# Twenty-three more identity products on TensorE around batch 0's second softmax

## The chip, the cores and the metric

The kernel runs on one core of a Trainium2 chip. The metric is the device time of one execution in microseconds, as the median over several runs. Beside it stands one profiled execution, whose trace gives each instruction's engine, start and duration. PE is TensorE, DVE VectorE, ACT ScalarE, POOL GpSimd, and SP the engine that issues the DMAs. PEld is TensorE's loading of weights.

## What is computed

Eight batches of eight heads, 576 tokens of 64 channels. Each head has 32 "packs" p, which first attend to the keys and values; the queries then attend to the packed result. What comes out, 4608 tokens of 512 channels, goes through a feed-forward layer with a hidden width of 2048.

```python
def sm_attn(qq, kk, vv):
    s = scale * np.matmul(qq, kk.transpose(0, 1, 3, 2))
    s = s - np.max(s, axis=-1, keepdims=True)
    a = np.exp(s)
    a = a / (np.sum(a, axis=-1, keepdims=True) + 1e-09)
    return np.matmul(a, vv)
p_packed = sm_attn(p, k, v)
out = sm_attn(q, p_packed, p_packed)
# x: out with its heads side by side, one row for each token
h = x @ w_in
g = h * (1.0 / (1.0 + np.exp(-h)))
return (g @ w_out).astype(np.float32)
```

The products that decide the length are done in three parts each: an operand is split into an upper and a lower half (`_hi`, `_lo`), and upper by upper, upper by lower and lower by upper are added up.

## The kernel before

For one batch the work goes like this. `scores1` multiplies packs by keys, `largest1`, `exps1` and `shares1` are the first softmax, `turned1` and `spread1` bring the exponentials to the other orientation, `packed` (L309) multiplies them by the values; for all batches but the first, `spread1` does its turn with 16 DMAs on SP (L288) behind two DVE transposes (L270). `scaled1`, `turned` and `packs` (L332, tile `ppT`) end this half. `scores2` multiplies queries by the packed result. For batch 0 it works in the orientation of the tokens (L350, in pieces of 32 columns), and then comes the second softmax in two halves: `less2` (the maximum, L387, and its subtraction, L388), `exps2` (L399 on ACT), `shares2` (sum L408, L409, L410, product L411), and `back2` turns the shares back by transposes on PE (L378, L380) into PSUM. `upper2` (L429, on ACT, tile `a_hi`) and `lower2` (L433, on DVE, tile `a_lo`) split them.

The packed result is not multiplied by the shares directly: `Packs` (`pp`) multiplies it by blocks of w_in (L211, `heads`, eight products), `pu` (L457 on ACT, `pw_hi`) and `pl` (L460 on DVE, `pw_lo`) split the result, and `h` (L488) multiplies shares and these blocks into hidden values; `g` (L506 to L508, ACT) applies the activation, `l` (L513, DVE) makes the lower half `g_lo`, and `o` (L520) multiplies by w_out into the output's sums. The weights come as 64-bit numbers and are taken apart and put together on ACT, DVE and POOL for the first 65 us or so (`ws`, `wz`, `wj`, `wu`, `wl`).

For the first two batches the order of all of this is written out by hand in the string `ORDER`: each word is a step, a letter or two for what it does, then its numbers. The words issue instructions on all the engines, and each engine runs its own in that order. `pp2`, `pu2`, `pl2` are the third block of packs; `aS0.0` is `scores2` of batch 0's first half, and `aM`, `aX`, `aD`, `aU`, `aH`, `aL` are `less2`, `exps2`, `shares2`, `back2`, `upper2`, `lower2`. A word `W` with a number n is `keep_warm(n)`:

```python
def two_banks():
    return ps_two.tile([P, 2, 512], F32, name="ps_two")
def keep_warm(n):
    ps = two_banks()
    for _ in range(n):
        nc.tensor.matmul(ps[:, 0, :P], ident, ident, start=True, stop=True)
```

That is n products of the 128x128 identity with itself into a PSUM tile that nobody reads (L132). Each of them shows as two records in the trace, as other f32 products do (L211, L309, L350). The pool `ps_two` has two buffers; the packs' products and the hidden products take theirs from it too. The kernel before has W2, W14, W12 and W5 in its first 20 us and W1 later.

Of the kernel before, what the change touches and what calls it, by code (L numbers as in the profile page):

```python
# [50 lines left out]
ORDER = """  # L51
wf0 ws0 wz0 k0 wf1 W2 wj0 as0.0 as0.1 wf2 ws1 am0.0 W14 ax0.0 am0.1 wf3 wz1 at0.0 v0 wj1 ax0.1 ay0.0 ws3 ws2
at0.1 W12 ay0.1 ar0 wz3 wu1 wz2 wj3 aa0 wf4 wj2 an0 W5 wl1 ai0 aj0 pp0 ws4 q0 pp1 wu3 wz4 pu0 aS0.0 wf5
aS0.1 wl3 wj4 wf6 wf7 pu1 pl0 pl1 aM0.0 wf8 pp2 pu2 aX0.0 pl2 ws7 aM0.1 k1 ws5 aD0.0 aX0.1 aU0.0 wf9 aD0.1
aU0.1 wz7 ws8 aH0.0 aL0.0 ws6 as1.0 aH0.1 wz8 wz5 ac1.0 q1 aL0.1 h0.0 wj5 wj7 as1.1 g0.0 ws9 ac1.1 h0.1 h1.0
l0.0 am1 g0.1 l0.1 wu5 o0.0 wu7 wz6 h1.1 g1.0 o0.1 v1 g1.1 wl5 wf10 l1.0 wl7 ax1.0 l1.1 wj6 o1.0 h2.0 ax1.1
o1.1 wz9 g2.0 wj8 h2.1 l2.0 at1.0 g2.1 pp3 pu3 pl3 at1.1 o2.0 l2.1 wj9 h3.0 ws10 o2.1 g3.0 ar1 h3.1 l3.0
wf11 ws11 pp4 o3.0 g3.1 pu4 wf12 wz10 ws12 l3.1 wj10 ay1 pl4 wz11 o3.1 wu10 wf13 h4 wj11 h5 wl10 g4 wu11 l4
aa1 o4 wz12 g5 an1 wl11 wf14 l5 ws13 ai1 aj1 h6 wj12 g6 wz13 aS1.0 o5 aT1.0 wj13 W1 ws14 h7 pp5 l6 o6 g7
wz14 aS1.1 wf15 pu5 l7 pl5 wj14 aT1.1 aM1.0 h8 g8 o7 wu14 wf16 k2 aM1.1 h9 ws15 l8 wl14 pp6 wz15 g9 aX1.0  # L60
aX1.1 wj15 l9 aD1.0 o8 h10 pu6 wu15 g10 pl6 o9 aH1.0 wl15 l10 v2 h11 o10 ws16 as2.0 g11 aL1.0 pp7 aD1.1
ac2.0 l11 pu7 as2.1 aH1.1 pl7 aL1.1 wf17 o11 h12 ws17 e11.0 g12 ac2.1 h13 e11.1 l12 g13 am2 h14 ax2.0 wz17
l13 wz16 h15 ax2.1 o12 g14 o13 l14 h16 wj16 g15 o14 l15 wj17 g16 wf18 ws18 h17 l16 o15 wz18 g17 l17 wf19
at2.0 h18 o16 at2.1 ws19 wj18 g18 h19 l18 o17 pp8 wu18 g19 q2 pu8 wz19 pl8 l19 ay2 o18 h20 g20 ar2 l20 o19
h21 wj19 o20 wl18 aa2 an2 g21 l21 pp9 h22 pu9 pl9 o21 h23 wu19 g22 l22 ai2 g23 aj2 wl19 o22 l23 h24 g24 o23
h25 aS2.0 l24 o24 g25 l25 aT2.0 h26 aS2.1 aM2.0 o25 g26 h27 l26 aT2.1 aM2.1 aX2.0 aX2.1 o26 pp10 g27 pp11 k3
pu10 aD2.0 l27 o27 pu11 pl10 pl11 e27.0 h28 e27.1 g28 l28 h29 g29 h30 v3 h31 o28 l29 aH2.0 aD2.1 aH2.1 o29
g30 l30 g31 l31 o30 g32 o31 aL2.1 l32 aL2.0 b0 e31.1 e31.0
"""


# [668 lines left out]
```

## Time and profile before

| | us |
|---|---|
| median of three runs | 716.32 |
| the three runs | 713.69, 716.32, 716.49 |
| the profiled execution | 713.68 |
| its span, first to last instruction | 711.9 |
| PE busy in the span | 695.0 |
| DVE busy | 332.7 |
| ACT busy | 325.0 |

A busy share is an average over stages with different limits, and the 712 us have two kinds of stage: the first 65 us, in which weights are prepared and attention of batches 0 and 1 is begun, and the rest. Where the change stands, the share of an engine in the stretch and the wait that ended last there have to be read. [...]

### The profile page before, as it was taken

The numbers are of one execution on the slowest core, as the hardware profiler recorded it, in microseconds if no ns is written. First come the engines' busy times: TensorE is split into PE (matmuls) and PEld (weight loads), VectorE is DVE, ScalarE is ACT, GpSimd is POOL, SyncE is SP. The second block draws the span as 40 slices with busy tenths as digits, with TensorE's granted clock in tenths as the row PEclk, the third lists the DMA queues.
The fourth block names the chain that finished last, engine by engine and source line by source line (L and its number), as shares of the span: only waits on it lengthen the run. The fifth ranks groups of instructions, "written<-read, shape, count | busy, mean of one in ns | idle before, by whom it ended". The sixth has DMA issues, their size and how long they took to land.

```text
span 711.9 us, 12319 instructions
## 1 busy us (share of the span) xinstructions
PE 695.0 (98%) x5170; PEld 570.4 (80%) x5170; DVE 332.7 (47%) x504; ACT 325.0 (46%) x612; POOL 18.7 (3%) x16
## 2 busy tenths in 40 slices
PE   7699999999999999999999999999999999999997
PEld 5477778887878887888878888878878888888886
DVE  5899986535543336332562325533362334622112
ACT  5597686434534425362542624453252532533221
POOL 1012110110000000000000000000000000000000
PEclk9789999999999999999999999999999999999999
DMA  9864714220512130212111121021301210010002
GB/s 341 355 229 129 293 65 188 87 71 1 185 60 82 34 139 0 100 44 89 67 60 54 43 90 68 21 106 35 137 1 60 82 35 1 1 60 1 1 1 74
DMA packets 30934, 62.07 MB, mean 87 GB/s; under 512 B 19360, under 2 KB 19360, under 8 KB 26528
## 3 DMA queue, kind: packets, MB, share of 16 engines
q1 hardware_dynamic: 30784, 61.16, 24.6%
q8 instruction: 41, 0.67, 0.4%
q10 hardware_dynamic: 96, 0.13, 0.1%
q14 instruction: 13, 0.11, 0.1%
HBM read 46.66 MB, written 10.49 MB: 80 GB/s over the span
## 4 chain that ended last, share of the span: by engine, by line
PE 94%; DVE 2%; SPq 1%; DMA 1%; issue 0%; ACT 0%; ACTq 0%
PE ps_acc L520 55%; PE ps_two L488 28%; PE ps_two L211 7%; PE ps_two L309 2%; SPq L288 1%; PE ps_two L132 1%; DMA kvq_t<-in_pkT 1%; PE ps_acc L350 1%; PE ps_acc L378 0%; DMA tm<-tm 0%; DVE g_lo L513 0%; PE ps_acc L309 0%; DVE tm L270 0%; DVE mx L247 0%; DVE w_raw L185 0%
## 5 line engine op out<-in xcount | busy, mean ns | idle before, releaser
L520 PE MATMUL ps_acc<-wo_hi,g_hi 128*128 128x512 f32 x576 | 229.3, 398 | 0.0
L520 PE MATMUL ps_acc<-wo_lo,g_hi 128*128 128x512 f32 x576 | 225.3, 391 | 0.0
L520 PE MATMUL ps_acc<-wo_hi,g_lo 128*128 128x512 f32 x576 | 225.0, 391 | 0.0
L513 DVE TENSOR_TENSOR g_lo<-g,g_hi 128x512 fp32r<-128x512 f32 (+1 forms) x132 | 90.9, 688 | 263.8 <-ACT g_hi L507 263.8
L506 ACT ACTIVATE g<-ps_two 128x512 f32<-128x512 f32 (+1 forms) x132 | 77.5, 587 | 275.8 <-PE ps_two L488 258.7
L488 PE MATMUL ps_two<-a_hi,pw_hi 128*128 128x288 f32 x512 | 153.2, 299 | 0.1
L488 PE MATMUL ps_two<-a_lo,pw_hi 128*128 128x288 f32 x512 | 152.0, 297 | 0.0
L488 PE MATMUL ps_two<-a_hi,pw_lo 128*128 128x288 f32 x512 | 151.2, 295 | 0.0
L520 PEld LDWEIGHTS ps_acc<-wo_hi,g_hi 128*128 128x128 f32 x576 | 108.0, 188 | 40.6 <-issue 21.0
L520 PEld LDWEIGHTS ps_acc<-wo_hi,g_lo 128*128 128x128 f32 x576 | 108.1, 188 | 24.0 <-DVE g_lo L513 0.5
L520 PEld LDWEIGHTS ps_acc<-wo_lo,g_hi 128*128 128x128 f32 x576 | 108.2, 188 | 18.2
L488 PEld LDWEIGHTS ps_two<-a_hi,pw_hi 128*128 128x128 f32 x512 | 96.9, 189 | 8.5 <-ACT rest L508 1.4
L488 PEld LDWEIGHTS ps_two<-a_lo,pw_hi 128*128 128x128 f32 x512 | 96.7, 189 | 3.6
L488 PEld LDWEIGHTS ps_two<-a_hi,pw_lo 128*128 128x128 f32 x512 | 96.7, 189 | 0.0
L507 ACT ACTIVATE g_hi<-ps_two 128x512 fp32r<-128x512 f32 (+1 forms) x132 | 76.6, 580 | 6.3 <-PE ps_acc L520 6.3
L460 DVE TENSOR_TENSOR pw_lo<-ps_two,pw_hi 128x1024 fp32r<-128x1024 f32 (+1 forms) x35 | 38.3, 1126 | 13.9 <-ACT pw_hi L457 13.9
L457 ACT CAST pw_hi<-ps_two 128x1024 fp32r<-128x1024 f32 (+1 forms) x35 | 31.7, 945 | 25.5 <-PE ps_two L211 25.5
L211 PE MATMUL ps_two<-win,ppT 64*32 64x512 f32 (+1 forms) x560 | 33.0, 559 | 1.1 <-issue 0.6
L508 ACT ACTIVATE rest<-ps_two 128x64 f32<-128x64 f32 (+1 forms) x132 | 30.2, 229 | 0.0
L211 PEld LDWEIGHTS ps_two<-win,ppT 64*32 64x32 f32 x560 | 8.2, 105 | 14.1 <-issue 11.2
L506 ACT ACT_TABLE_LOAD x15 | 19.2, 1283 | 0.5 <-PE ps_two L488 0.4
L498 ACT CAST g_hi<-rest 128x512 fp32r<-128x512 f32 x16 | 9.9, 624 | 14.5 <-PE ps_acc L520 14.2
(98 smaller groups left out, 446.3 us busy)
## 6 DMA issues: line engine op xcount, KB each, us to landing
kvq_t<-in_pkT SPq DMA_DIRECT2D x7, 1216.0 KB, 6.7
kvq_t<-in_vA SPq DMA_DIRECT2D x8, 1024.0 KB, 5.3
out<-o SPq DMA_DIRECT2D x16, 512.0 KB, 2.8
kvq_t<-in_qT SPq DMA_DIRECT2D x7, 1152.0 KB, 5.6
w_raw<-in_w_in SPq DMA_DIRECT2D x6, 1024.0 KB, 6.3
win<-in_w_out SPq DMA_DIRECT2D x3, 1024.0 KB, 4.9
w_raw<-in_w_out SPq DMA_DIRECT2D x3, 1024.0 KB, 4.8
tm<-tm SPq DMA_DIRECT2D x56, 40.0 KB, 2.0
```

What stands on the lines that cost most here:

```text
L132: nc.tensor.matmul(ps[:, 0, :P], ident, ident, start=True, stop=True)
L211: nc.tensor.matmul(bank(par)[NP * i : NP * i + NP], lhs(r, i), rhs(r, i), start=True, stop=True)
L309: nc.tensor.matmul(self.ps[NP * i : NP * i + NP, par * D : par * D + D], e, v[:n, c, h * D : h * D + D], start=(c == 0), stop=(c == 4),)
L457: nc.scalar.copy(self.hi, self.ps[:, :, : self.nf * P])
L460: nc.vector.tensor_tensor(self.lo, self.ps[:, :, : self.nf * P], self.hi.bitcast(F32), ALU.subtract)
L488: nc.tensor.matmul(bank, p[:, par, cols], a[:, par], start=(n == 0), stop=(n == len(todo) - 1))
L498: nc.scalar.copy(g_hi, g)
L506: nc.scalar.activation(g, ps[..., :MAIN], AF.Silu)
L507: nc.scalar.activation(g_hi, ps[..., :MAIN], AF.Silu)
L508: nc.scalar.activation(to, ps[..., MAIN:HS], AF.Silu)
L513: nc.vector.tensor_tensor(g_lo[:, c], g[:, c], g_hi[:, c].bitcast(F32), ALU.subtract)
L520: nc.tensor.matmul(bank, g[:, rows], w[:, f], start=(first and n == 0), stop=(last and n == 2))
```

## The change

Two words are put into `ORDER`: `W4` behind `wf8`, ahead of `pp2` (the third block of packs), and `W19` behind `aX0.1`, ahead of `aU0.0` (the transposes of the first half's shares). All other words stay in their order; the lines below are only broken in other places.

```diff
-aS0.1 wl3 wj4 wf6 wf7 pu1 pl0 pl1 aM0.0 wf8 pp2 pu2 aX0.0 pl2 ws7 aM0.1 k1 ws5 aD0.0 aX0.1 aU0.0 wf9 aD0.1
-aU0.1 wz7 ws8 aH0.0 aL0.0 ws6 as1.0 aH0.1 wz8 wz5 ac1.0 q1 aL0.1 h0.0 wj5 wj7 as1.1 g0.0 ws9 ac1.1 h0.1 h1.0
+aS0.1 wl3 wj4 wf6 wf7 pu1 pl0 pl1 aM0.0 wf8 W4 pp2 pu2 aX0.0 pl2 ws7 aM0.1 k1 ws5 aD0.0 aX0.1 W19 aU0.0 wf9
+aD0.1 aU0.1 wz7 ws8 aH0.0 aL0.0 ws6 as1.0 aH0.1 wz8 wz5 ac1.0 q1 aL0.1 h0.0 wj5 wj7 as1.1 g0.0 ws9 ac1.1
...
```

On PE, from the end of batch 0's second scores (L350) to its transposes (L378), this is the piece of the difference, with what each instruction waits for:

```order
 L350 MATMUL ps_acc<-ppT,kvq_t 128x32 x16
+L132 MATMUL ps_two<-ident 128x128 [waits DVE_49]
+L132 MATMUL ps_two<-ident 128x128 x3
 L211 MATMUL ps_two<-win,ppT 32x128 [waits DVE_49]
 L211 MATMUL ps_two<-win,ppT 32x128 x7
-L378 MATMUL ps_acc<-ident,tm 128x128 [waits DVE_49,PE_49]
+L132 MATMUL ps_two<-ident 128x128 [waits PE_49]
+L132 MATMUL ps_two<-ident 128x128 x18
+L378 MATMUL ps_acc<-ident,tm 128x128 [waits DVE_49]
 L378 MATMUL ps_acc<-ident,tm 128x128
```

The four products stand ahead of the block of packs (L211) and the nineteen behind it; the first of the four waits for DVE (its buffer was read by an earlier `pl`), the first of the nineteen for PE itself.

On DVE nothing moves; these are the rows, in both kernels, from the first half's maximum to the first half's shares. `pl2` is the row of L460:

```order
L387 TENSOR_REDUCE on_tokens<-ps_acc 128x24 [waits PE_49]
L388 TENSOR_TENSOR tm<-ps_acc,on_tokens 128x768 [waits DVE_49]
L460 TENSOR_TENSOR pw_lo<-ps_two,pw_hi 128x2x128 [waits Activation_49]
L387 TENSOR_REDUCE on_tokens<-ps_acc 128x16
L388 TENSOR_TENSOR tm<-ps_acc,on_tokens 128x2x256 [waits DVE_49]
L408 TENSOR_REDUCE on_tokens<-tm 128x24 [waits Activation_49]
L409 TENSOR_SCALAR on_tokens<-on_tokens 128x24 [waits DVE_49]
L410 RECIPROCAL on_tokens<-on_tokens 128x24 [waits DVE_49]
L411 TENSOR_TENSOR tm<-tm,on_tokens 128x768 [waits DVE_49]
```

The second half's maximum (the second L387) stands behind `pl2`, which waits for ACT's `pu2` and through it for the third block of packs on PE; L411 at the end is what the transposes wait for. On ACT, POOL and SP the order is the same in both kernels.

## Rows read from the trace of the kernel before

**Rows 1.** The page: busy time of PE; granted clock in 40 slices, in tenths.

```profile
PE 695.0 (98%) x5170; PEld 570.4 (80%) x5170; DVE 332.7 (47%) x504; ACT 325.0 (46%) x612; POOL 18.7 (3%) x16
...
PEclk9789999999999999999999999999999999999999
```

**Rows 2.** Waits of PE, whole span: us in total, times, longest.

```profile
PE ps_acc L378 <- DVE tm L411: 4.8, 1, 4.8
...
PE ps_two L309 <- DMA tm<-tm: 1.3, 1, 1.3
```

**Rows 3.** Stretches: length, busy time (and instructions) of each engine, clock, DMA share, GB/s.

```profile
25.70:26.27 0.57, 0.00 (x0) 0.00 (x1) 0.00 (x0) 0.00 (x0) 0.00 (x0) 1.00 1.08 455
...
26.81:27.20 0.39, 0.00 (x0) 0.00 (x0) 0.00 (x0) 0.39 (x2) 0.00 (x0) 0.79 0.95 399
...
31.51:36.17 4.66, 4.60 (x29) 2.06 (x29) 4.49 (x9) 3.56 (x6) 0.00 (x0) 0.50 0.31 126
36.17:40.70 4.53, 4.53 (x36) 3.29 (x29) 4.46 (x9) 4.33 (x7) 1.77 (x2) 0.50 0.10 22
...
27.22:51.93 24.71, 20.25 (x129) 14.78 (x130) 24.16 (x43) 23.03 (x45) 2.33 (x2) 0.73 0.63 238
```

The engines in these rows are PE, PEld, DVE, ACT and POOL, in this order.

**Rows 4.** All waits of DVE from 27 to 66 us.

```profile
DVE pw_lo L460 <- ACT pw_hi L457: 1.8, 1, 1.8
```

**Rows 5.** The chain that ended last, at the start of L309: start, us, what.

```profile
61.83 1.91 DMA tm<-tm
63.74 0.14 issue
63.87 1.68 PE ps_two L309 x74
```

**Rows 6.** SP's issues of line 288 up to 66 us: ns each, first and last start.

```profile
L288 SPq DMA_DIRECT2D tm<-tm x16: 594/600/738, 52.0 to 61.8; - x16
```

**Rows 7.** Later stretches, columns as in rows 3.

```profile
66.00:80.00 14.00, 13.86 (x102) 10.26 (x107) 13.83 (x20) 9.02 (x15) 0.00 (x0) 1.00 0.70 254
...
120.00:300.00 180.00, 179.96 (x1308) 147.14 (x1307) 79.04 (x117) 77.14 (x146) 4.64 (x2) 1.00 0.24 82
```

**Rows 8.** The chain that ended last, round the third block of packs.

```profile
13.87 2.68 PE ps_two L132 x24
...
25.36 0.33 PE ps_two L211 x2
25.70 0.57 issue
26.27 0.52 PE ps_two L211 x14
```

**Rows 9.** Timeline, DVE's pw_lo and PE's product with it: start, us, instruction.

```profile
57.42 1.22 DVE L460 TENSOR_TENSOR pw_lo<-ps_two,pw_hi 128x1024 fp32r<-128x1024 f32 x1
...
58.76 0.33 PE L488 MATMUL ps_two<-a_hi,pw_lo 128*128 128x288 f32 x1
```

**Rows 10.** DMA queues from 20 to 30 us: packets, MB, share of 16 engines.

```profile
q8 instruction: 1, 0.02, 0.7%
```

**Rows 11.** The page: the instruction queue over the whole span.

```profile
q8 instruction: 41, 0.67, 0.4%
```

**Rows 12.** Timeline from 31 to 42 us: transposes, a_hi and a_lo, and L488.

```profile
31.51 0.66 PE L378 MATMUL ps_acc<-ident,tm 128*128 128x128 f32 x2 [4.79 <-DVE tm L411]
...
33.30 0.64 ACT L429 CAST a_hi<-ps_acc 128x576 fp32r<-128x576 f32 x1 [0.65 <-PE ps_acc L380]
...
34.17 0.75 DVE L433 TENSOR_TENSOR a_lo<-ps_acc,a_hi 128x576 fp32r<-128x576 f32 x1
...
37.05 0.44 PE L488 MATMUL ps_two<-a_hi,pw_hi 128*128 128x288 f32 x1
...
37.29 0.44 PE L488 MATMUL ps_two<-a_lo,pw_hi 128*128 128x288 f32 x1
...
41.10 0.29 PE L488 MATMUL ps_two<-a_hi,pw_hi 128*128 128x288 f32 x1
41.23 0.29 PE L488 MATMUL ps_two<-a_lo,pw_hi 128*128 128x288 f32 x1
```

More of the change, by code (lines that the diff above doesn't have):

```diff
@@ L53 @@
 at0.1 W12 ay0.1 ar0 wz3 wu1 wz2 wj3 aa0 wf4 wj2 an0 W5 wl1 ai0 aj0 pp0 ws4 q0 pp1 wu3 wz4 pu0 aS0.0 wf5
-aS0.1 wl3 wj4 wf6 wf7 pu1 pl0 pl1 aM0.0 wf8 pp2 pu2 aX0.0 pl2 ws7 aM0.1 k1 ws5 aD0.0 aX0.1 aU0.0 wf9 aD0.1
-aU0.1 wz7 ws8 aH0.0 aL0.0 ws6 as1.0 aH0.1 wz8 wz5 ac1.0 q1 aL0.1 h0.0 wj5 wj7 as1.1 g0.0 ws9 ac1.1 h0.1 h1.0
-l0.0 am1 g0.1 l0.1 wu5 o0.0 wu7 wz6 h1.1 g1.0 o0.1 v1 g1.1 wl5 wf10 l1.0 wl7 ax1.0 l1.1 wj6 o1.0 h2.0 ax1.1
-o1.1 wz9 g2.0 wj8 h2.1 l2.0 at1.0 g2.1 pp3 pu3 pl3 at1.1 o2.0 l2.1 wj9 h3.0 ws10 o2.1 g3.0 ar1 h3.1 l3.0
@@ L58 @@
[L58 to L67, printed above, removed]
@@ L68 @@
-g30 l30 g31 l31 o30 g32 o31 aL2.1 l32 aL2.0 b0 e31.1 e31.0
+aS0.1 wl3 wj4 wf6 wf7 pu1 pl0 pl1 aM0.0 wf8 W4 pp2 pu2 aX0.0 pl2 ws7 aM0.1 k1 ws5 aD0.0 aX0.1 W19 aU0.0 wf9
+aD0.1 aU0.1 wz7 ws8 aH0.0 aL0.0 ws6 as1.0 aH0.1 wz8 wz5 ac1.0 q1 aL0.1 h0.0 wj5 wj7 as1.1 g0.0 ws9 ac1.1
+h0.1 h1.0 l0.0 am1 g0.1 l0.1 wu5 o0.0 wu7 wz6 h1.1 g1.0 o0.1 v1 g1.1 wl5 wf10 l1.0 wl7 ax1.0 l1.1 wj6 o1.0
+h2.0 ax1.1 o1.1 wz9 g2.0 wj8 h2.1 l2.0 at1.0 g2.1 pp3 pu3 pl3 at1.1 o2.0 l2.1 wj9 h3.0 ws10 o2.1 g3.0 ar1
+h3.1 l3.0 wf11 ws11 pp4 o3.0 g3.1 pu4 wf12 wz10 ws12 l3.1 wj10 ay1 pl4 wz11 o3.1 wu10 wf13 h4 wj11 h5 wl10
@@ new lines @@
+g4 wu11 l4 aa1 o4 wz12 g5 an1 wl11 wf14 l5 ws13 ai1 aj1 h6 wj12 g6 wz13 aS1.0 o5 aT1.0 wj13 W1 ws14 h7 pp5
+l6 o6 g7 wz14 aS1.1 wf15 pu5 l7 pl5 wj14 aT1.1 aM1.0 h8 g8 o7 wu14 wf16 k2 aM1.1 h9 ws15 l8 wl14 pp6 wz15 g9
+aX1.0 aX1.1 wj15 l9 aD1.0 o8 h10 pu6 wu15 g10 pl6 o9 aH1.0 wl15 l10 v2 h11 o10 ws16 as2.0 g11 aL1.0 pp7
+aD1.1 ac2.0 l11 pu7 as2.1 aH1.1 pl7 aL1.1 wf17 o11 h12 ws17 e11.0 g12 ac2.1 h13 e11.1 l12 g13 am2 h14 ax2.0
+wz17 l13 wz16 h15 ax2.1 o12 g14 o13 l14 h16 wj16 g15 o14 l15 wj17 g16 wf18 ws18 h17 l16 o15 wz18 g17 l17
@@ new lines @@
+wf19 at2.0 h18 o16 at2.1 ws19 wj18 g18 h19 l18 o17 pp8 wu18 g19 q2 pu8 wz19 pl8 l19 ay2 o18 h20 g20 ar2 l20
+o19 h21 wj19 o20 wl18 aa2 an2 g21 l21 pp9 h22 pu9 pl9 o21 h23 wu19 g22 l22 ai2 g23 aj2 wl19 o22 l23 h24 g24
+o23 h25 aS2.0 l24 o24 g25 l25 aT2.0 h26 aS2.1 aM2.0 o25 g26 h27 l26 aT2.1 aM2.1 aX2.0 aX2.1 o26 pp10 g27
+pp11 k3 pu10 aD2.0 l27 o27 pu11 pl10 pl11 e27.0 h28 e27.1 g28 l28 h29 g29 h30 v3 h31 o28 l29 aH2.0 aD2.1
+aH2.1 o29 g30 l30 g31 l31 o30 g32 o31 aL2.1 l32 aL2.0 b0 e31.1 e31.0
```

## The prediction

> **What bounds the kernel now.** The page first: TensorE (PE) is busy for 695.0 of 711.9 us, and its clock line is below nine tenths in two slices of 40, both in the first 54 us [rows 1]. Then PE's waits: the longest one is 4.8 us, ahead of the transposes at L378, for VectorE's L411; once the first data are in, the only other one over half a microsecond that ends with another engine's work is 1.3 us ahead of L309, for a DMA [rows 2]. [...] From 31.51 to 40.70 PE is busy for 4.60 + 4.53 us, all at the half level. That is what the change aims at: 9.1 us of PE work that would take some 4.6 at the full level.
>
> What the work of those microseconds is worth is read from the wait that ends last behind them. Three views tell it. VectorE (DVE) has one wait in the 39 us from 27 to 66, the 1.8 us that end at 27.21, where pl2 (L460) waits for ScalarE's pw_hi and so for the third block of packs [rows 4]. From there to the end of the second L270 transpose at 51.93 it is busy for 24.16 of 24.71 us, while PE has 20.25 [rows 3]. Behind L270 stands SP's queue: 16 DMA issues of L288 one after the other, the first at 52.0 and the last at 61.8, a landing of 1.91 us, and only then PE's L309 at 63.87, which is where PE has waited 1.3 us [rows 2, 5, 6]. So the date at which batch 1's packed attention starts on PE is set by DVE and SP, not by PE. Behind it PE has no wait worth the name: 13.86 of 14 us busy to 80 us, 179.96 of 180 from 120 to 300 [rows 7]. From 63.87 on the kernel is bound by PE; from 27.21 to 63.87 by DVE and SP; and what PE does at half clock in between lies beside them.
>
> **W19 and the clock.** In the trace, 12 identity products (24 records, two for each) take 2.68 us on the chain [rows 8], so one takes 0.223 us at the full clock, and 19 take 4.24 us. They stand behind the third block of packs. If that ends at 27.5 (next part), they run from 27.5 to 31.7, and the transposes, which wait for L411 and start at 31.51 now [rows 12], would start at about 32.2, since L411 comes 0.7 later (next part too). So W19 fits into the wait with half a microsecond to spare, and nothing is queued behind it on PE but those transposes. I expect the full clock to hold from there. W19's wait on PE's own earlier products costs nothing, since they stand ahead of it in the same queue.
>
> What it frees: the transposes, scores and first hidden products between 31.5 and 40.7 go up to twice as fast, and PE then stops for DVE's results, which come no earlier. Where PE's work after the stretch meets DVE's, the room is small in the trace of before: pw_lo, that begins at 57.42 and takes 1.22, ends at 58.64, and PE's product with it starts at 58.76 [rows 9]. Whatever PE gains before, at most some 0.1 us of it is left there, and at L309 nothing, since the DMA lands when it lands. Term of the gain: 0.
>
> **W4 and the chain.** Four products stand between the scores of batch 0 and the third block of packs, that is ahead of the one thing DVE waits for. Without a stall they would push it by 4 x 0.223 = 0.89 us. But there is a stall in the trace just here: PE does two records of that block (25.36 to 25.70), stands 0.57 us for nothing that the profile shows ("issue"), and does the other 14 from 26.27 to 26.79 [rows 8]. What becomes of this stall decides the price.
> - If it stands at that count of PE instructions and ends at 26.27 whatever is there, the first identity product runs ahead of it, three behind it, and then the whole block: 3 x 0.223 = 0.67, and one pack product more than the seven that stood behind it, 0.52 us / 14 x 2 = 0.07 [rows 8]. Together 0.74 us: the block ends at about 27.5 in place of 26.8.
> - If it belongs to the block's own second product and only ends at a set time, W4 runs inside it: 25.36 + 0.89 + 8 x 0.07 = 26.81 against 26.79: nothing.
> - If it follows the block with its full length, or there is none in either kernel, 0.89 us.
>
> I take 0.74, since the stall has the look of a fetch of instructions: nothing else waits there, weight loads stand as well, one packet of the instruction queue moves between 20 and 30 us, and the DMA engines are full through the stall, 1.08 of their time [rows 3, 10]. The page's 41 packets of that queue bring 0.67 MB [rows 11]; they are 16 KB each, and PE's 5170 products and as many weight loads [rows 1] make about 252 instructions for each, so its place goes by count.
>
> [...]
>
> Who pays: pu2 on ACT and pl2 on DVE start 0.74 us later, and with pl2 everything queued behind it on DVE (the second half's maximum L387, then L388, L408 to L411, and on to L270), since the queue is in order and has no gap to take it up [rows 4]; so do SP's 16 issues and L309. The wait of PE ahead of L309 grows by what PE still has in hand, and the end moves by 0.74 us.
>
> **The sum.** Gain 0, W4 +0.7, W19 0. The profiled execution took 713.68 us (span 711.9, 1.8 around it), so it would be 714.4. The three timed runs are at 713.69, 716.32 and 716.49: the profiled one stands with the lowest, 2.6 below the median. One trace does not tell what makes these 2.7 us, and I know no reason why the change would take them away, so against the median I expect 716.32 + 0.7 = 717.0.
>
> **Rivals.**
> *The clock pays as aimed.* If PE set the date of L309, the end would come forward by half of 9.1, less W4: -4.6 + 0.7 = -3.9, so 712.4, or 711.7 without W4's price. For it: the half level is in the rows, and W19 is dense work in just the idle stretch. Against it: DVE's 24.16 of 24.71, and a PE that already waits 1.3 us at L309 [rows 2, 3]. It would take a DVE that runs faster when PE does, and no row shows one. Chance 0.05. [...]
>
> *The clock falls all the same* (slower). It fell within 0.4 us of the end of PE's last product [rows 3], at the head of the idle stretch, so the sparse work ahead of it (scores in 64x32 pieces, the 0.57 us stall) may be what counted, and W4 adds only 0.9 us there. Then W19 runs at the half level: one product as L488's go, 0.24 from one start to the next at half against 0.13 at full [rows 12], so 0.223 x 0.24 / 0.13 = 0.41 us, and 19 take 7.8, from 27.5 to 35.3 in place of 32.2. DVE's a_lo (L433) had 0.23 us of room (a_hi ends at 33.94, a_lo starts at 34.17 [rows 12]), so DVE is 3.1 - 0.2 = 2.9 us late, with W4 3.6: 716.32 + 3.6 = 719.9. It decides as soon as W19 ends after 32.45, that is at (32.45 - 27.5) / 19 = 0.26 us or more for a product. If the clock comes back within W19, as dense products make likely (it came back at 40.7 in the trace, behind 4.53 us of PE work without a gap [rows 3]), what is left is between 0.7 and 2.3. Chance 0.10, 0.04 of it for the full price.
>
> *The clock falls at the wait for L309.* PE now arrives there with idle spots behind it, and from L309 on every microsecond of dense work at the half level costs half of it. Before, a wait of 1.3 us there did not bring the clock down [rows 2], and the page's clock line is at nine or more from the fourth slice on [rows 1]. Were there a stretch like that from 27.2 to 40.7, 13.5 us at half, and all of it dense work, it would cost 6.7 us: 723; one of a third of that, 2.3 us. Chance 0.05.
>
> *The change does not reach the path*: W4 vanishes in the stall, 716.4 us. Chance 0.13.
>
> **How the numbers follow.** Forecast case 0.67. Range: from the lowest run with W4 nearly hidden, 713.69 + 0.2 = 713.9, to the highest run with a late W19 whose clock comes back, 716.49 + 2.3 = 718.8. About 0.5% (3.6 us) is what a measurement of this kernel tells from no change. Forecast, hidden W4 and most of the part-late W19 lie within it: 0.67 + 0.13 + 0.06, and of the first rival and the last clock rival some 0.02, so 0.88. Faster 0.04; slower 0.04 (W19 at half) + 0.04 (cold behind L309) = 0.08.
>
> **What would show it.** Right, if the clock of 27.2 to 40.7 reads 1.00; W19 takes 4.2 us and ends before L411; the third block of packs ends near 27.5 and DVE's wait for pw_hi grows from 1.8 to 2.5; PE's lost time turns into waits for DVE between 32 and 41; and L309's second group starts near 64.6 by the span, where DVE again has no other wait. Wrong, if L309 starts before 63.8, if DVE shows a wait between 28 and 52, if the stall at 25.70 moves or goes, or if a slice behind 64 us shows less than the full clock.

## The result

The changed kernel takes 719.4 us, the median of 22 runs (715.09 to 720.66); the kernel before takes 715.5, the median of as many (713.35 to 716.49). The ratio, which goes by the means, is 1.0048, with a 95% interval from 1.0034 to 1.0061: the change costs 3.4 us (the medians lie 3.9 apart), and the forecast range ended at 718.8. The direction (a small loss, and no gain from the clock) was as forecast; the size was five times the 0.7 us of the sum. The 22 runs are of three kinds: four at 715.1 to 715.6 with a mean clock of 0.995, three at 717.2 to 717.9 (0.992 or 0.993) and fifteen at 718.6 to 720.7 (0.990 or 0.991), to which the profiled one belongs.

The profiled execution of the changed kernel took 719.01 us, 717.2 in its span. Its busy times on the page, against those of [rows 1]:

```profile
span 717.2 us, 12410 instructions
...
PE 702.9 (98%) x5216; PEld 579.2 (81%) x5216; DVE 333.0 (46%) x504; ACT 324.9 (45%) x612; POOL 18.6 (3%) x16
```

46 more PE records, and 7.9 us more of PE's busy time. Most of it is the 23 products themselves: 2.0 for W4, as the chain below shows, and 5.4 for W19, from the end of the third block of packs (29.42) to 34.83. PE's timeline (start, us, instruction):

```profile
28.66 0.68 PE L211 MATMUL ps_two<-win,ppT 64*32 64x128 f32 x16
29.27 5.56 PE L132 MATMUL ps_two<-ident 128*128 128x128 f32 x38
34.66 0.38 PE L378 MATMUL ps_acc<-ident,tm 128*128 128x128 f32 x2
```

The stretches of the changed kernel that answer to [rows 3] (length; busy time and count of PE, PEld, DVE, ACT, POOL; granted clock as a share, 1.00 the full level and 0.50 the half level; DMA share, GB/s):

```profile
24.60:26.70 2.10, 2.10 (x23) 2.04 (x21) 1.25 (x2) 0.00 (x0) 0.00 (x0) 0.52 1.00 415
26.70:28.73 2.03, 2.03 (x18) 1.81 (x24) 0.00 (x0) 0.00 (x0) 0.00 (x0) 0.50 1.00 417
...
31.50:34.70 3.20, 3.20 (x31) 3.20 (x30) 3.06 (x7) 3.20 (x6) 0.00 (x0) 1.00 0.49 204
...
41.70:45.20 3.50, 3.31 (x13) 2.77 (x12) 3.43 (x8) 3.21 (x9) 2.19 (x2) 0.51 0.68 274
...
65.70:68.25 2.55, 0.06 (x1) 0.03 (x1) 2.55 (x2) 0.25 (x1) 2.27 (x1) 1.00 0.68 171
...
69.00:72.50 3.50, 3.50 (x53) 2.74 (x46) 3.31 (x5) 3.12 (x6) 0.00 (x0) 0.51 0.25 103
```

The one long stretch at the half level has become three. In the kernel before the clock reads 1.00 to the end of the third block of packs and 0.50 from 27.2 to 40.7 us:

```profile
24.50:26.79 2.29, 1.64 (x32) 1.07 (x30) 0.95 (x1) 0.00 (x0) 0.00 (x0) 1.00 1.01 418
...
27.20:40.70 13.50, 9.13 (x56) 5.38 (x57) 13.10 (x24) 12.20 (x19) 1.77 (x2) 0.50 0.46 185
```

Of the three stretches of the changed kernel the first begins at 24.7, in the middle of batch 0's scores, before W4 has started, and ends inside W19. The second is at 41.7 to 45.2. The third is behind L309, where PE has no other limit; the stretch ahead of it is PE's idle wait for the DMA.

The chain of waits of the changed kernel, against [rows 8] and [rows 5] (start, us, what):

```profile
21.12 5.60 PE ps_acc L350 x118
26.72 2.00 PE ps_two L132 x8
28.73 0.69 PE ps_two L211 x16
...
29.44 0.38 ACT pw_hi L457
...
29.85 0.42 DVE pw_lo L460
...
33.04 0.96 DVE tm L411
...
54.24 0.69 DVE tm L270
...
64.84 3.27 DMA tm<-tm
...
68.25 2.23 PE ps_two L309 x74
70.48 3.90 PE ps_acc L520 x12
```

W4's eight records take 2.00 us and stand on the chain. pl2 starts at 29.85 in place of 27.21, 2.6 us later; the second L270 ends 3.0 later (54.93 against 51.93), L309's second group starts 4.4 later (68.25 against 63.87), and the 86 records behind it take 6.13 us. In the kernel before they take 4.64: 1.68 for L309 [rows 5] and, next on its chain, 2.95 for L520:

```profile
65.55 2.95 PE ps_acc L520 x12
```

All waits of VectorE from 20 to 70 us, against [rows 4], and two of PE's, against [rows 2] (us in total, times, longest):

```profile
DVE pw_lo L460 <- ACT pw_hi L457: 4.0, 1, 4.0
DVE g_lo L513 <- ACT g_hi L507: 0.3, 1, 0.3
```

```profile
PE ps_two L309 <- DMA tm<-tm: 2.5, 1, 2.5
...
PE ps_two L488 <- ACT rest L508: 1.3, 1, 1.3
```

VectorE's wait for pw_hi has grown from 1.8 to 4.0 us, and a short one for g_hi has come. It does not wait for a_hi. PE's wait of 4.8 us for L411 is gone; a part of the time that it gains between 34.7 and 41 is back as a wait of 1.3 us ahead of h0.1.

### The profile page after: what moved, and what is told of

Its sections match the earlier page's. It is cut to its first block, busy times and chain, and to the rows that moved or that the text cites. A ratio compares the mean times of both kernels' runs of the same rounds, so it can differ in the third digit from the quotient of the medians.

```text
span 717.2 us, 12410 instructions
## 1 busy us (share of the span) xinstructions
PE 702.9 (98%) x5216; PEld 579.2 (81%) x5216; DVE 333.0 (46%) x504; ACT 324.9 (45%) x612; POOL 18.6 (3%) x16
## 4 chain that ended last, share of the span: by engine, by line
PE 93%; DVE 3%; SPq 1%; DMA 1%; issue 0%; ACT 0%; ACTq 0%
PE ps_acc L520 55%; PE ps_two L488 28%; PE ps_two L211 6%; PE ps_two L309 2%; PE ps_two L132 1%; SPq L288 1%; DMA kvq_t<-in_pkT 1%; PE ps_acc L350 1%; DMA tm<-tm 0%; DVE w_raw L185 0%; PE ps_acc L309 0%; DVE tm L411 0%; DVE win L191 0%; DVE on_tokens L408 0%; DVE win L185 0%
## 5 line engine op out<-in xcount | busy, mean ns | idle before, releaser
L520 PE MATMUL ps_acc<-wo_hi,g_hi 128*128 128x512 f32 x576 | 230.0, 399 | 0.0
L520 PE MATMUL ps_acc<-wo_lo,g_hi 128*128 128x512 f32 x576 | 225.9, 392 | 0.0
L520 PE MATMUL ps_acc<-wo_hi,g_lo 128*128 128x512 f32 x576 | 225.3, 391 | 0.0
L488 PE MATMUL ps_two<-a_hi,pw_hi 128*128 128x288 f32 x512 | 152.9, 299 | 1.5 <-ACT rest L508 1.3
L488 PE MATMUL ps_two<-a_lo,pw_hi 128*128 128x288 f32 x512 | 151.9, 297 | 0.0
L488 PE MATMUL ps_two<-a_hi,pw_lo 128*128 128x288 f32 x512 | 151.1, 295 | 0.0
L520 PEld LDWEIGHTS ps_acc<-wo_hi,g_hi 128*128 128x128 f32 x576 | 108.5, 188 | 40.7 <-issue 21.1
L520 PEld LDWEIGHTS ps_acc<-wo_hi,g_lo 128*128 128x128 f32 x576 | 108.5, 188 | 24.1 <-DVE g_lo L513 0.5
L520 PEld LDWEIGHTS ps_acc<-wo_lo,g_hi 128*128 128x128 f32 x576 | 108.6, 189 | 18.2
L488 PEld LDWEIGHTS ps_two<-a_hi,pw_hi 128*128 128x128 f32 x512 | 96.6, 189 | 9.2 <-ACT rest L508 2.3
L488 PEld LDWEIGHTS ps_two<-a_lo,pw_hi 128*128 128x128 f32 x512 | 96.4, 188 | 3.9 <-DVE a_lo L433 0.2
L488 PEld LDWEIGHTS ps_two<-a_hi,pw_lo 128*128 128x128 f32 x512 | 96.6, 189 | 0.0
L460 DVE TENSOR_TENSOR pw_lo<-ps_two,pw_hi 128x1024 fp32r<-128x1024 f32 (+1 forms) x35 | 38.3, 1126 | 16.0 <-ACT pw_hi L457 16.0
L457 ACT CAST pw_hi<-ps_two 128x1024 fp32r<-128x1024 f32 (+1 forms) x35 | 31.7, 945 | 27.7 <-PE ps_two L211 27.7
L211 PE MATMUL ps_two<-win,ppT 64*32 64x512 f32 (+1 forms) x560 | 32.8, 563 | 0.5 <-DVE ppT L332 0.4
L132 PE MATMUL ps_two<-ident 128*128 128x128 f32 x114 | 17.9, 321 | 1.4 <-POOL ident masks.py:199 1.4
L132 PEld LDWEIGHTS ps_two<-ident 128*128 128x128 f32 x114 | 16.7, 231 | 2.9 <-POOL ident masks.py:199 1.4
```

Source lines behind the costliest of these rows:

```text
L211: nc.tensor.matmul(bank(par)[NP * i : NP * i + NP], lhs(r, i), rhs(r, i), start=True, stop=True)
L457: nc.scalar.copy(self.hi, self.ps[:, :, : self.nf * P])
L460: nc.vector.tensor_tensor(self.lo, self.ps[:, :, : self.nf * P], self.hi.bitcast(F32), ALU.subtract)
L488: nc.tensor.matmul(bank, p[:, par, cols], a[:, par], start=(n == 0), stop=(n == len(todo) - 1))
L520: nc.tensor.matmul(bank, g[:, rows], w[:, f], start=(first and n == 0), stop=(last and n == 2))
```

## The experiments

All are edits of the word list `ORDER`. Each kernel was run beside the kernel before on the same chip, and the ratios are against that. The question of the first four was which of the two words costs what, and whether the half level behind L309 is part of it.

**W4 alone.**

```diff
-wf8 pp2 pu2 aX0.0 pl2
+wf8 W4 pp2 pu2 aX0.0 pl2
```

> The kernel before with W4 alone (no W19). Theory A: W4 on the chain is the cost. The changed kernel's third block of packs ends 2.6 us later than before, because the clock is already at its half level when W4 runs (2.0 us for four products) and VectorE waits for that block; then W4 alone costs 1 to 2.5 us over before, and most of the 3.9 us between the two medians (715.5 and 719.4). Theory B: W19 is the cost, by making TensorE early, so that it stands idle ahead of L309 and its clock is at half behind it (3.4 us at half in the changed kernel's trace, some 1.7 us); then W4 alone costs under 1 us and the clock behind L309 stays full. Theory C: the two profiled executions only differ in where the clock steps, and neither word costs anything: ratio 1.000 within its interval.

Measured: 716.39 us (11 runs) against 714.78; ratio 1.0023 (1.0014 to 1.0032), 1.6 us. The chain and VectorE's only wait:

```profile
26.77 2.00 PE ps_two L132 x8
```

```profile
DVE pw_lo L460 <- ACT pw_hi L457: 4.0, 1, 4.0
```

W4 takes 2.00 us here too, and VectorE's wait is the 4.0 us of the changed kernel. Theory A holds for W4, but it is half of the loss and not most of it. The half level lasts from 24.7 to 41.7, one stretch as in the kernel before, and there is none behind L309.

**W19 alone.**

```diff
-aD0.0 aX0.1 aU0.0 wf9 aD0.1
+aD0.0 aX0.1 W19 aU0.0 wf9 aD0.1
```

> The kernel before with W19 alone (no W4). Theory A: W19 fits in the wait for L411 and costs nothing: the same as before within 1 us, and VectorE's wait for the third block of packs as before. Theory B: most of the 3.9 us come from here: 1.5 to 3 us over before, with a stretch at the half level behind 64 us. Theory C: ratio 1.000.

Measured: 716.17 us (11 runs, 715.53 to 719.87); ratio 1.0030 (1.0016 to 1.0044). Theory A is wrong: W19 is not free. Theory B comes nearer (2.1 us by the ratio, 1.4 by the medians), but this trace has no half level behind 64 us. The chain, the clock and VectorE's waits behind W19:

```profile
27.76 6.53 PE ps_two L132 x38
34.29 0.22 PE ps_acc L378 x2
...
42.96 2.56 PE ps_acc L520 x6
```

```profile
25.30:32.10 6.80, 6.80 (x52) 6.25 (x51) 4.67 (x8) 4.25 (x8) 0.00 (x0) 0.50 1.02 423
```

```profile
DVE g_lo L513 <- ACT g_hi L507: 0.7, 1, 0.7
DVE a_lo L433 <- ACT a_hi L429: 0.7, 1, 0.7
```

Nineteen products take 6.53 us and not 4.24, since two thirds of that time lie at the half level. They end at 34.29, the transposes that they hold up had been free since 32.40 (L411 ends there), and VectorE waits 0.7 us for what comes of them. W19 has a second effect: from 42.4 to 45.7 the clock is at the half level again, where the kernel before is at the full level (its long stretch ended at 40.7). Six records of L520 take 2.56 us there, they stand on the chain, and VectorE waits another 0.7 us, for the g_hi that follows them.

Besides, the eleven runs fall into two groups: eight at 715.5 to 717.2 with a mean clock of 0.993, three at 718.8 to 719.9 with 0.990. In the changed kernel 15 of 22 runs are like these three, 718.6 to 720.7 at 0.990 or 0.991, the profiled one among them, with its third stretch at the half level. A mean clock tells how much of a run lay at the half level and not where; that the other runs at 0.990 have a stretch behind L309 too is inferred.

**All 23 products behind the third block of packs.**

```diff
-aD0.0 aX0.1 aU0.0 wf9 aD0.1
+aD0.0 aX0.1 W23 aU0.0 wf9 aD0.1
```

> All 23 products behind the third block of packs (W23 ahead of the transposes, nothing ahead of the block): as many products as in the change, at the other place. Theory A: the place is what costs; the same as W19 alone, within 1 us of before, unless the products run at the half level (0.41 us each, 9.4 us) and hold up the transposes, which would give 1 to 3 us. Theory B: as much slower as the change, or more (3 to 4 us). Theory C: ratio 1.000.

Measured: 718.52 us (6 runs); ratio 1.0045 (1.0027 to 1.0063), 3.2 us, as much as the change. VectorE's wait for the block is the 2.0 us of W19 alone, so W4's price is gone, and another has come in its place:

```profile
28.01 7.49 PE ps_two L132 x46
35.50 0.22 PE ps_acc L378 x2
```

```profile
DVE a_lo L433 <- ACT a_hi L429: 1.6, 1, 1.6
```

Four products more behind the block hold up the transposes by 1.2 us more. So it is not the place alone: each of the two places has its own price. Three of the six runs are at 719.2 to 719.7 with a mean clock of 0.989 or 0.990; the profiled one, at 717.35, has no half level behind L309.

**The changed kernel with W7 ahead of batch 1's packed attention.**

```diff
-l4 aa1 o4
+l4 W7 aa1 o4
```

> The changed kernel with seven more identity products in the wait ahead of batch 1's packed attention (W7 ahead of aa1, 1.6 us at the full clock, where the changed kernel's TensorE waited 2.5 us for the DMA). It asks what the half level behind L309 costs. If that stretch (69.0 to 72.5 us in the changed kernel's trace) is on the path and comes of the idle wait, the time falls by 1 to 1.7 us against the changed kernel, to a median of about 718; if it is not, or if the idle wait does not bring it, the time stays at 719.4 or rises by up to 1 us.

Measured: 717.79 us (5 runs, 717.0 to 718.27, all at a mean clock of 0.992 or 0.993); ratio 1.0038 (1.0025 to 1.0051). No run is of the 0.990 kind any more, where 15 of 22 had been. In its trace PE is busy where the changed kernel's stood still, and the clock stays full behind L309:

```profile
46.70:69.00 22.30, 22.14 (x183) 18.15 (x182) 21.37 (x30) 17.61 (x34) 4.64 (x2) 1.00 0.58 175
69.00:73.00 4.00, 4.00 (x63) 3.24 (x56) 3.97 (x6) 3.12 (x5) 0.00 (x0) 1.00 0.55 231
```

So with the idle wait ahead of L309 filled, the half level behind it did not come in this trace (1.00 from 69 to 73 us), and where it lies in the changed kernel, from 69.0 to 72.5, PE is busy for 3.50 of 3.50 us, so the kernel is bound by PE there and pays for it. What W7 saves, 0.7 us by the ratios, is rough: the two intervals overlap.

The next four ask whether VectorE's and SP's chain is really what sets the date of L309, as the prediction had it, and whether W4 and W19 have prices apart from that.

**No products, but pl2 out of VectorE's way.**

```diff
-pp2 pu2 aX0.0 pl2 ws7 aM0.1 k1 ws5 aD0.0 aX0.1
+pp2 aX0.0 pu2 ws7 aM0.1 k1 ws5 aD0.0 pl2 aX0.1
```

> The kernel before, without any of the 23 products, but with the third block's pl2 taken out of VectorE's way: pl2 stands behind the first half's shares (L411) and not ahead of the second half's maximum, and pu2 behind the first exponential on ScalarE. VectorE then has nothing to wait for in the 1.8 us ahead of pl2. Theory A (from 25 to 64 us VectorE and SP set the date of L309, and TensorE's clock there does not matter): 1 to 1.8 us faster than before, though the half level stays as it is. Theory B (TensorE at its half level sets it): no change, within 0.5 us.

Measured: 713.33 us (7 runs, 712.06 to 713.79) against 715.23; ratio 0.9975 (0.9964 to 0.9985). VectorE's wait is 0.8 us, and for the scores themselves, and the half level is as long as ever:

```profile
DVE on_tokens L387 <- PE ps_acc L350: 0.8, 1, 0.8
```

```profile
24.90:38.50 13.60, 9.95 (x84) 5.84 (x82) 12.43 (x23) 10.85 (x19) 0.00 (x1) 0.50 0.61 252
```

Theory A: the time follows VectorE's wait, and 13.6 us at the half level beside it cost nothing that can be seen.

**The same with W4.**

```diff
-wf8 pp2 aX0.0 pu2
+wf8 W4 pp2 aX0.0 pu2
```

> The same with W4 ahead of the third block of packs. W4 alone cost 1.6 us over before by the medians. Theory A: its price is VectorE's longer wait for the block and nothing else, so here, where nothing behind it waits, it costs under 0.5 us against the kernel without it (e5_pl2_later). Theory B: its price lies on TensorE itself or in a later half level; then it costs its 1.6 us here too.

Measured: 715.12 us (12 runs); ratio 1.0009 (0.9996 to 1.0022), 1.8 us over the kernel without W4. My expectation of under 0.5 us was wrong. VectorE's wait had only moved:

```profile
DVE on_tokens L408 <- ACT tm L399: 1.7, 1, 1.7
```

pl2 no longer stands in VectorE's way, but pu2 still stands in ScalarE's, ahead of the second exponential, and it waits for the same late block. The profiled run took 716.45 us, one of five at 716.4 to 718.5; the other seven are at 714.3 to 715.2. Its trace has a half level behind L309, though there is no W19 here and PE's wait for the DMA is no longer than the 1.3 us of [rows 2] (a stretch with columns as above, then the wait):

```profile
66.60:70.00 3.40, 3.40 (x34) 2.49 (x23) 3.37 (x5) 3.19 (x5) 0.00 (x0) 0.50 0.51 212
```

```profile
PE ps_two L309 <- DMA tm<-tm: 1.3, 1, 1.3
```

**The changed kernel with pl2 moved.** The same two steps moved in the changed kernel.

> The changed kernel, W4 and W19 in place, with the same two steps moved as in e5_pl2_later. Theory A: W4's part of the loss goes, and W19's grows, since VectorE's L411 is done some 2 to 4 us earlier and the transposes now stand behind W19, which ends where it did: 716 to 718 us, 2 to 4 us over e5_pl2_later. If W19 were free, it would be as fast as e6_pl2_later_w4 within 0.5 us.

Measured: 719.55 us (6 runs); ratio 1.0051 (1.0034 to 1.0067), 4.4 us over e6_pl2_later_w4 and 6.2 over e5_pl2_later by the medians, more than I had expected. Four of the runs are at 719.5 to 719.7 with a mean clock of 0.989 or 0.990; the other two, the profiled one among them, are at 716.8 with 0.992 or 0.993, and the trace has no half level behind L309. In it W19 ends at 34.97, where e5_pl2_later starts its transposes at 30.7, and VectorE waits 1.7 us for the exponential and 1.1 for a_hi. The chain:

```profile
29.24 5.73 PE ps_two L132 x38
```

The wait for a_hi is longer than the 0.7 of W19 alone, and ScalarE's second exponential still stands behind pu2. But the two runs at 716.8 lie within Theory A's 716 to 718 and only 1.7 us over the median of e6_pl2_later_w4; the rest of the 4.4 lies in the four others, of which no trace was kept.

**W10 in W19's place, no W4.**

```diff
-aD0.0 aX0.1 aU0.0 wf9 aD0.1
+aD0.0 aX0.1 W10 aU0.0 wf9 aD0.1
```

> The kernel before with W10 in W19's place and no W4: short enough to end ahead of L411 at the half level too (ten products of 0.41 us from 27.5 are over at 31.6). W19 alone cost 1.4 us by the medians, with VectorE 0.7 us late for a_hi in its trace. If the lateness of the transposes is the price, W10 costs under 0.4 us over before and VectorE does not wait for a_hi. If the price is that TensorE is early and then cold behind L309, W10 still shows runs of 718 us and over, as W19 alone did in 3 of 11.

Measured: 715.29 us (12 runs, 713.47 to 716.49); ratio 1.0000 (0.9990 to 1.0010). Ten products end ahead of L411, PE still waits 0.9 us for it, VectorE does not wait for a_hi, and the cost is nil. No run is over 718. The trace has a short half level behind L309 all the same (66.9 to 70.3, behind a wait of 1.3 us), and it shows what that costs there, where the kernel before has 2.95 us for the same 12 records:

```profile
66.86 4.55 PE ps_acc L520 x12
```

The last four close the two accounts.

**pl2 moved, with W7 ahead of L309.**

```diff
-l4 aa1 o4
+l4 W7 aa1 o4
```

> e5_pl2_later (pl2 behind the first half's shares, no products added at the second softmax) with W7 in the wait ahead of batch 1's packed attention. In the changed kernel W7 there took the time from 719.4 to 717.8 and left no run with a third stretch at the half level. Theory: what W7 saves is that stretch and nothing else; e5_pl2_later showed it in no run (713.33, mean clocks 0.989 to 0.992), so W7 changes the time here by less than 0.5 us either way. If W7 is of use in itself, 712.5 or under; if it delays L309, 714 or over.

Measured: 713.37 us (10 runs); ratio 0.9975 (0.9966 to 0.9983), the same as without W7. So W7 saves a stretch at the half level where there is one, and nothing else.

**pu2 and pl2 behind all of the softmax.**

```diff
-pp2 pu2 aX0.0 pl2 ws7 aM0.1 k1 ws5 aD0.0 aX0.1 aU0.0 wf9 aD0.1
-aU0.1
+pp2 aX0.0 ws7 aM0.1 k1 ws5 aD0.0 aX0.1 pu2 aU0.0 wf9 aD0.1
+pl2 aU0.1
```

> The kernel before with pu2 behind both exponentials on ScalarE and pl2 behind both halves' shares on VectorE, no products added: the control for the next kernel. With W4 put into e5_pl2_later the time rose by 1.8 us and VectorE waited 1.7 us for the second exponential, which stood behind pu2 on ScalarE. Expected as e5_pl2_later, 713.3 within 0.7 us.

Measured: 713.31 us (12 runs, one of which took 1746 us and is unexplained); ratio 0.9979 (0.9970 to 0.9989), as e5_pl2_later.

**The same with W4.**

```diff
-wf8 pp2 aX0.0 ws7
+wf8 W4 pp2 aX0.0 ws7
```

> e10_pu2_later with W4 ahead of the third block of packs. Theory A: W4's price is the lateness of the block for whatever stands behind it in a queue (VectorE's pl2 in the change, ScalarE's pu2 in e6_pl2_later_w4); with both moved behind the softmax's steps nothing waits, and W4 costs under 0.5 us against e10_pu2_later. Theory B: W4 costs its 1.6 to 1.8 us here too, so the price lies on TensorE.

Measured: 713.13 us (6 runs, 711.80 to 713.21); ratio 0.9966 (0.9954 to 0.9978). W4 costs nothing. It still runs at the half level and the block still ends late (timeline: start, us, instruction), but now nobody waits for it, and VectorE's only wait is 0.4 us for the scores:

```profile
26.49 2.23 PE L132 MATMUL ps_two<-ident 128*128 128x128 f32 x8
28.64 0.68 PE L211 MATMUL ps_two<-win,ppT 64*32 64x128 f32 x16
30.56 0.66 PE L378 MATMUL ps_acc<-ident,tm 128*128 128x128 f32 x2 [1.24 <-DVE tm L411]
```

```profile
DVE on_tokens L387 <- PE ps_acc L350: 0.4, 1, 0.4
```

**W19 with W7 ahead of L309, no W4.**

```diff
-aD0.0 aX0.1 aU0.0 wf9 aD0.1
+aD0.0 aX0.1 W19 aU0.0 wf9 aD0.1
-l4 aa1 o4
+l4 W7 aa1 o4
```

> W19 without W4, with W7 in the wait ahead of batch 1's packed attention. W19 alone had runs at 715.5 to 717.2 us (mean clock 0.993) and three at 718.8 to 719.9 (0.990). Theory: W19's price is two things, the transposes held up (0.7 us of waiting for a_hi on VectorE in its trace) and, in the runs at 0.990, the half level behind L309; W7 takes away the second, so that no run is over 718 and the median stays 0.5 to 1.5 us over before. If runs at 0.990 and over 718 us remain, the idle wait ahead of L309 is not what brings the half level.

Measured: 715.96 us (11 runs, 714.72 to 716.76, mean clocks 0.992 to 0.995); ratio 1.0010 (1.0002 to 1.0019), 0.7 us. No run is over 718. VectorE's wait for a_hi is 0.5 us and that for g_hi 0.7. W19's price has two parts: some 0.7 us are left here, with these two waits, and W7 takes away the rest of the 2.1 us of W19 alone, for the half level behind L309 that is inferred there from the mean clocks.

Together, by the ratios: W4 1.6 us, W19 through VectorE's waits 0.7, the half level behind L309 between 0.7 (the changed kernel's ratio against that with W7) and 1.4 (W19 without and with W7). That is 3.0 to 3.7 us, and the change costs 3.4. The intervals of these ratios are 1.2 to 2.0 us wide, and the parts come from different kernels: in the changed kernel's own trace, in which W4 makes VectorE late already, it does not wait for a_hi and waits 0.3 us for g_hi. So the sum shows that nothing large is missing, and not each part to a tenth.

## Why the prediction was wrong

**The gain of 0 held.** What PE does at half clock between 25 and 41 us lies beside VectorE's and SP's work. In the changed kernel PE is at the full level from 31.5 to 41.7 and L309 starts no earlier; in e5_pl2_later it is at half for 13.6 us and the kernel is 1.9 us faster than before, by the medians, because VectorE's wait is shorter. The rival "the clock pays as aimed" is out.

**W4's path held, its size did not.** With pl2 and pu2 out of the way W4 costs nothing (e11_pu2_later_w4), so its price is the lateness of the block for the queues behind it. The step that failed is the price of one product, "0.223 us at the full clock". It came from W12 at 14 us, where the clock reads 1.00, and the prediction took the clock at W4's place from a single execution, in which it was full until 26.8 [rows 3]. In the changed kernel the clock falls at 24.7, and it does so without the change too: e2_w19_only, e5_pl2_later, e8_w10_only and e9_pl2_later_w7 are, up to the third block of packs, the same PE program as the kernel before, and in their traces the half level begins at 25.3, 24.9, 26.0 and 24.5 (and in e3_w23_behind, e10_pu2_later and e12_w19_w7, of which the same holds, at 25.7, 26.0 and 25.0). Those of the first two are shown above; of the third and fourth, in this order, a stretch at the fall (columns as above):

```profile
26.00:26.70 0.70, 0.70 (x10) 0.70 (x8) 0.55 (x1) 0.00 (x0) 0.00 (x0) 0.50 0.98 413
```

```profile
24.40:25.00 0.60, 0.60 (x10) 0.60 (x9) 0.56 (x2) 0.00 (x0) 0.00 (x0) 0.57 1.02 428
```

So the profiled execution of before was the odd one: its fall came last, behind the block. In all six traces with W4 the fall lies between 24.7 and 26.2, ahead of W4, which starts at 26.5 to 26.9 and so runs at the half level. Ten products behind the fall take 4.63 us in e8_w10_only (timeline, 27.98 to 32.61; clock 0.50 as they begin), so one takes 0.46 and four 1.85; W4's 2.00 is that and 0.15. The eight traces of one PE program up to the block, with falls from 24.5 to 27.0, show that the place of this step varied from trace to trace.

The stall of 0.57 us [rows 8] is not gone either. In three of the seven other traces without W4 it is still behind the block's second record; the first two records then count as busy through it, but PE's weight loads show the gap. The timeline of e8_w10_only:

```profile
26.76 0.18 PEld L211 LDWEIGHTS ps_two<-win,ppT 64*32 64x32 f32 x2
...
26.77 1.28 PE L211 MATMUL ps_two<-win,ppT 64*32 64x128 f32 x16
...
27.37 0.22 PEld L211 LDWEIGHTS ps_two<-win,ppT 64*32 64x32 f32 x14 [0.43 <-issue]
```

e10_pu2_later and e3_w23_behind have the same gap at the same record, 0.45 and 0.23 us; in the other four the loads have none, and the block takes 0.81 to 0.96 us. Behind W4 it takes 0.68. That the stall stays with the count of instructions, as the prediction took it, is not shown by these: with W4 the loads of its four products have no such gap, and only the 0.15 us are left for it (0.3 in e11_pu2_later_w4). Nor is it shown that the stall is a fetch of instructions, as the prediction estimated from the packets of the instruction queue. Its length differs from trace to trace, and what sets that was not tried. In all, ScalarE's pw_hi, which follows the block, starts at 27.4 to 28.1 in the six traces of the experiments in which it waits for the block without W4 (26.8 in the kernel before, whose block ran ahead of the fall), and at 29.4 to 29.7 in the five with W4: about 1.2 to 2.3 us later, which holds the 1.6 that W4 alone costs.

**W19's step failed in the same place.** The prediction let it end at 31.7, half a microsecond ahead of the transposes. It ended at 34.8 in the changed kernel, where W4 let it start 1.9 us later than forecast (29.4), and at 34.3 alone; in both it begins at the half level and takes 5.4 and 6.5 us in place of 4.24. The rival "the clock falls all the same" had this, with the condition right (over 0.26 us for a product; it was 5.4 us / 19 = 0.28 in the changed kernel and 6.53 / 19 = 0.34 alone) and the clock coming back within W19; its chance of 0.10 was far too low. Its price was put at 0.7 to 2.3 with W4 in it: W19's part without the half level behind L309 measured 0.7 (e12_w19_w7), and W4's 1.6, together the top of that range. The prediction had no term for the half level coming back behind 41.7; in the six traces with W19 or W23 it did, and VectorE waited 0.3 to 0.7 us for g_hi.

**The third rival came on top.** "The clock falls at the wait for L309" had a chance of 0.05 and, by the mean clocks, happened in about two thirds of the runs (15 of 22). The prediction argued from one trace that the kernel before has a wait of 1.3 us there and no fall. The changed kernel's profiled wait was 2.5 us, but in e6_pl2_later_w4 and e8_w10_only the fall came behind 1.3 us as well. Its price, 1.5 us in the changed kernel's trace (6.13 in place of 4.64), was within the 2.3 that the prediction gave for a short stretch. The rivals were treated as alternatives, one price each; they are parts of the same course of things and their prices add up, and that is what put the time beyond the range.

**What stays open.** 1.4 of the 4.4 us by which L309 was late in the changed kernel's profile are a DMA landing of 3.27 us in place of 1.91; in the other traces here whose chain shows it, it took 1.89 to 2.55. Why it was late was not tried. Nor is it known what decides on the fall behind L309: with the wait filled by W7 it did not come (1.00 from 69 to 73 us in e4_after_w7_packed), but a wait of 1.3 us had it in two traces and not in seven others (the kernel before, e1_w4_only, e2_w19_only, e5_pl2_later, e7_after_pl2_later, e10_pu2_later, e11_pu2_later_w4), and 1.6 us in e3_w23_behind had none. What in the scores brings the first fall was not tried either. And four runs of the changed kernel, at a mean clock of 0.995, took 715.1 to 715.6 us, no longer than the kernel before; no trace of such a run was kept, so the prices above are those of the executions in which the clock falls as in the traces shown.

## What to carry to other kernels

A clock step read off one trace is one draw (here it lay between 24.5 and 27.0 us in eight traces): before a product is priced at the level that its place shows, look at the same place in several executions, and price it at the other level too when the time of the step moves across it. Filler ahead of an instruction that another engine's in-order queue waits for was paid by that queue here (1.6 us for four products that took 2.0); the cheaper cure was to take the waiting steps out of the queues: with pu2 and pl2 behind the softmax the kernel is 1.8 us faster than before by the medians, with no filler at all. And rivals that can happen together need the sum of their prices in the range.

## What was not expected of the hardware

The same 16 records (batch 0's first scores here, batch 1's there) take 1.22 us at 6.3 us, where the clock reads 1.00, 1.21 at 35 us at the half level, and 0.72 in the changed kernel at 37 us at the full level. From the kernel before, and then from the changed kernel:

```profile
6.31 1.22 PE L211 MATMUL ps_acc<-kvq_t 64*32 64x288 f32 x16 [3.73 <-DMA kvq_t<-in_pkT]
...
35.02 1.21 PE L211 MATMUL ps_two<-kvq_t 64*32 64x288 f32 x16
```

```profile
36.95 0.72 PE L211 MATMUL ps_two<-kvq_t 64*32 64x288 f32 x16
```

So the first products go at the pace of the half level (1.22 us, as 1.21 there), although the clock reads full. That the reading is wrong at the start of a trace is inferred from these durations and was not tried.

The half level came back 10.2 us after W19 had seen it end, at 41.7, with PE busy for 8.66 of those 10.2 us:

```profile
31.50:41.70 10.20, 8.66 (x85) 6.32 (x84) 9.89 (x19) 9.76 (x17) 0.13 (x1) 1.00 0.28 87
```

So filling one idle stretch did not keep the clock up. The work that it let run early left idle spots of its own further on, 1.3 us ahead of h0.1 the longest; that these brought the fall is argued and not shown.
